# Last output tiles of part B run among the prepass's first chains, later loads of fresh stores, and the gate values in fewer transfers

## The chip, the core and the metric

The kernel runs on one core of one Trainium2 chip. The metric is device microseconds of one execution, as the median over several runs; less is better. The core has a matmul engine (TensorE, PE in the profile, with its weight loads as PEld), three engines for elementwise work (VectorE, DVE; ScalarE, ACT; GpSimd, POOL), and SyncE (SP), which here only issues DMA transfers. ACT issues some transfers too. On each engine's queue instructions start in order: one that waits holds up all behind it.

## The reference

Two attention layers over the same x (2048 positions, 640 features) are mixed by a gate, g*a + (1-g)*b.

```python
g = sigmoid((x * gate_w).sum(-1, keepdims=True))
# A: 32 heads of 192, a memory of 8 rows carried from segment to segment
for s in range(64):
    h = concat([mem, x[:, 32*s:32*s+32]])
    q, k, v = h @ Wq, h @ Wk, h @ Wv            # 640 -> 32 x 192 each
    p = softmax(where(mask, q @ k.T * 192**-0.5, -1e9))
    o = einsum('bhte,hed->btd', p @ v, Wo)
    mem, out = o[:, :8], o[:, 8:]
# B: 32 heads of 20, each position looks at 8 positions, 2 apart
q, k, v = split(x @ wqkv)
p = softmax(where(idx >= 0, q . k[pos - 2*w] * 20**-0.5, -1e9))   # w = 0..7
b = (p . v[pos - 2*w]) @ wo
return g * a + (1 - g) * b
```

Inputs and weights are bf16.

## The kernel before

The program runs in three stages. **Part B** (`part_b`, L91 to L465) computes the local attention, scales its output by 1-g and stores it in DRAM (`bsc_dram`), for part A to add. The **prepass** (`prepass`) projects the rows that part A needs of all 64 segments at once (zTi, the last 8 positions of each segment) with the weights of part A and stores them (`zpk_dram`). **Part A** then goes through the 64 segments one after the other.

*Part B* works in five blocks of 484 positions (the last has 112). A block has eight steps, each for one group g of four heads; the last block has two steps of four groups each. A step makes the scores on PE (L260) from `bqkT`, the exponentials on ACT (L267), the band mask on DVE (L276), then, one step later, the sums and values on PE (`ps_bZ`, `ps_bO`, L292), their reciprocal as two activations on ACT (L305, L306), and the product on DVE (L324), which after each four groups is stored to `bo_dram` by four transfers (L328).

Between these, jobs for the next block are taken: transposes of x (`xT_chain`, L160), the gate (`gate`, which also loads the next x tiles), projections to q and k (`proj`, L227; evacuated to `bqkD`, four buffers; stored to `bqk_dram`, L234), projections to v (`v_chain`, L210), and output chains of the block before (`out_chain`, L345). q and k come back in another layout through DRAM: `load_qk` (L243) reads `bqk_dram` into `bqkT`, half a block by four transfers. The attention output goes the same way: `load_o` (L333) reads `bo_dram` into `OT`, and an `out_chain` for one tile `ti` of 128 positions and one half `f` of the features is five matmuls of 128x320, an evacuation with the factor 1-g (`omg_sb`; ACT for f=0, L348; DVE for f=1, L350) into `bo` (two buffers), and after f=1 a store to `bsc_dram` (L352). There are 16 tiles, so 32 chains.

The gate values go through DRAM as well: `g_sb` to `g_dram` (L375), then four loads to `gA` (L385) and sixteen loads of 32x1 to `gZ` (L390), two transfers after each step from block 2 on.

In part B the order on PE, ACT, DVE and SP is the order in which the code records it (`manual_schedule`). On SP stand besides the above: early weights of part A (`wres_*`, L538), copies of some weights in DRAM (`wscr`, L524), and the first segment. PE has eight banks of PSUM; part B uses two for jobs (`b_psm`), four for scores and two for `ps_bO` and `ps_bZ`.

*Between part B and the prepass*, `load_late(0)` asks on SP for thirty weight slices (13 `wlate_k`, 16 `wlate_v`, one `wlate_oa`, 384 KB each, L538). From here a scheduler places the instructions in each engine's order.

*The prepass* calls `project_qk` four times (p = 0 to 3). Each has 24 chains of five matmuls 128x512 (L583), evacuated in turn by ACT (L77) and DVE (L79) into `ZS`, which one transfer on ACT's queue stores (L587, 3072 KB). ZS lies in the pool `zs0` for p = 0 and 2, in `zs1`, on the right side of SBUF, for p = 1 and 3. Then `project_v` (L595) with stores at L604. The prepass takes PSUM from a pool of eight banks.

PSUM and SBUF pools are freed and taken again; an instruction that writes to space of a closed pool waits for what still uses it.

Of the kernel before, what the change touches and what calls it, by code (L numbers as in the profile page):

```python
# [27 lines left out]
class _K:  # L28
# [61 lines left out]
    def part_b(self):  # L90
# [9 lines left out]
        self.xh_dram = self.dram.tile([S // 32, 128, KC * 32], BF, name="xh_dram")  # L100
        self.gA = self.const.tile([128, 4 * self.NT], F32, name="gA")
        self.gZ = self.const.tile([128, 4], F32, name="gZ")
        with ExitStack() as ctx:
            wp = ctx.enter_context(tc.tile_pool(name="b_w", bufs=1))
            io = ctx.enter_context(tc.tile_pool(name="b_io", bufs=4))
            blkp = ctx.enter_context(tc.tile_pool(name="b_blk", bufs=1))
            wk = ctx.enter_context(tc.tile_pool(name="b_wk", bufs=2))
            psm = ctx.enter_context(tc.tile_pool(name="b_psm", bufs=2, space=bass.MemoryType.PSUM))
            psS = ctx.enter_context(tc.tile_pool(name="b_psS", bufs=2, space=bass.MemoryType.PSUM))
            psO = ctx.enter_context(tc.tile_pool(name="b_psO", bufs=1, space=bass.MemoryType.PSUM))  # L110

# [11 lines left out]
                load_x(i)  # L123
            wv = wp.tile([128, KC, 640], BF, name="wv_sb")
            gw = wp.tile([128, KC, 1], BF, name="gw_sb")
            wo = wp.tile([128, KC, 640], BF, name="b_wo")
            wqk = [wp.tile([128, KC, 640], BF, name=f"b_w{n}") for n in "qk"]
            xT = wp.tile([128, KC, HALO + S], BF, name="xT")
            OT = wp.tile([128, KC, S], BF, name="OT")
            wsrc = self.wqkv.rearrange("(c p) f -> p c f", p=128)  # L130
            nc.sync.dma_start(wqk[0][:], wsrc[:, :, 0:640])
            nc.scalar.dma_start(wqk[1][:], wsrc[:, :, 640:1280])
# [14 lines left out]
            nc.vector.memset(xT[:, :, 0:HALO], 0.0)  # L147
            gz = wp.tile([128, self.NT], F32, name="gz_sb")
            g_sb = wp.tile([128, self.NT], F32, name="g_sb")
            omg_sb = wp.tile([128, self.NT], F32, name="omg_sb")  # L150
            sel_ones = wp.tile([128, 160], BF, name="sel_ones")
            zTi = self.zTi.rearrange("p c (i s) -> p c i s", i=8)
            heads = lambda t: t.rearrange("(g h d) n -> h d g n", h=4, d=20)
# [10 lines left out]
            def gate(b):  # L164
                t0 = 512 * b
                for i in range(4):
                    del xs[4 * b + i]
                    if 4 * b + 4 + i < self.NT:
                        load_x(4 * b + 4 + i)
                ps_g = bank(F32, "ps_g")  # L170
                for i in range(4):
                    c0 = HALO + t0 + 128 * i
                    for kc in range(KC):
                        nc.tensor.matmul(ps_g[:, i:i + 1], lhsT=xT[:, kc, c0:c0 + 128], rhs=gw[:, kc, :],
                                         start=(kc == 0), stop=(kc == KC - 1), skip_group_check=True)
                gs = slice(4 * b, 4 * b + 4)
                nc.scalar.activation(gz[:, gs], ps_g[:, 0:4], ACT.Exp, scale=-1.0)
                nc.vector.tensor_scalar_add(gz[:, gs], gz[:, gs], 1.0)
                nc.vector.reciprocal(g_sb[:, gs], gz[:, gs])
                nc.vector.tensor_scalar(out=omg_sb[:, gs], in0=g_sb[:, gs], scalar1=-1.0, scalar2=1.0,  # L180
                                        op0=ALU.mult, op1=ALU.add)
                xv = xT[:, :, HALO + t0:HALO + t0 + 512].rearrange("p c (s t) -> p s c t", t=32)
                xh = blkp.tile([128, 16, KC, 32], BF, name="xh_blk")
                nc.gpsimd.tensor_copy(xh[:, :, :, 8:32], xv[:, :, :, 0:24])
                nc.gpsimd.tensor_copy(xh[:, :, :, 0:8], xv[:, :, :, 24:32])
                xh_stores.append(lambda: nc.sync.dma_start(
                    self.xh_dram[16 * b:16 * b + 16].rearrange("s p f -> p s f"), xh[:].rearrange("p s c t -> p s (c t)")))
                z_copy = nc.gpsimd.tensor_copy(zTi[:, :, :, 16 * b:16 * b + 16],
                                               xv[:, :, :, 24:32].rearrange("p s c i -> p c i s"))
                if b == 3:  # L190
                    with tc.issue_after(z_copy.ins):
                        self.build_sel(self.const, sel_ones[:])
# [137 lines left out]
            def load_o(b):  # L330
                nq, nu, c0 = shape_of(b)
                nt = nq * nu
                load = nc.sync.dma_start(OT[:, :, BQ * b:BQ * b + nt], ot_dram[b][:].rearrange("(c p) n -> p c n", p=128))  # L333
                if b == 2:
                    self.mid_load = load.ins

# [1 line left out]

            def out_chain(ti, f):
                if f == 0:  # L340
                    bos[ti] = io.tile([128, 640], BF, name="bo", bufs=2)
                bo = bos[ti]
                ps = bank(F32, "ps_bo")
                for c in range(KC):
                    nc.tensor.matmul(ps[:, 0:320], lhsT=OT[:, c, 128 * ti:128 * ti + 128],  # L345
                                     rhs=wo[:, c, 320 * f:320 * f + 320], start=(c == 0), stop=(c == KC - 1))
                if f == 0:
                    nc.scalar.activation(bo[:, 0:320], ps[:, 0:320], ACT.Copy, scale=omg_sb[:, ti:ti + 1])  # L348
                else:
                    nc.vector.tensor_scalar(out=bo[:, 320:640], in0=ps[:, 0:320], scalar1=omg_sb[:, ti:ti + 1],  # L350
                                            scalar2=None, op0=ALU.mult)
                    nc.sync.dma_start(self.bsc_dram[ti * 128:(ti + 1) * 128, :], bo[:])  # L352
# [4 lines left out]
            with order:  # L357
# [12 lines left out]
                for u in range(4):  # L370
                    for f in range(2):
                        v_chain(0, u, f)
                    if u == 0:
                        load_qk(0, 1)
                misc, misc_g = [], [lambda: nc.sync.dma_start(g_dram[:].rearrange("u t n -> (u t) n"), g_sb[:])]  # L375

                def load_first():
                    self.hT0 = self.load_seg(0)
# [5 lines left out]
                for jj in range(4):  # L384
                    misc_g.append(lambda jj=jj: nc.sync.dma_start(  # L385
                        self.gA[32 * jj:32 * jj + 32, :].rearrange("t (u n) -> t u n", u=4),
                        g_dram[:].rearrange("u t n -> t u n")))
                for n in range(4):
                    for q in range(4):
                        misc_g.append(lambda n=n, q=q: nc.sync.dma_start(  # L390
                            self.gZ[32 * q:32 * q + 32, n:n + 1], g_dram[:, 24:32, 4 * n + q:4 * n + q + 1]))

                steps = [(b, (g,)) for b in range(NB - 1) for g in range(8)]
                steps += [(NB - 1, tuple(range(4 * n, 4 * n + 4))) for n in range(2)]
# [1 line left out]

                def add_outs(b):
                    load_o(b)
                    later.extend([lambda ti=ti, f=f: out_chain(ti, f) for ti in range(self.NT) for f in range(2)
                                  if BQ * b < 128 * (ti + 1) <= BQ * b + BQ])  # L400

                for i, (b, gs) in enumerate(steps):
                    g, nb, jobs = gs[0], b + 1, []
# [17 lines left out]
                    for _ in range(n_out.get(g, 0) if nb < NB else 1 + 2 * (i == len(steps) - 1)):  # L421
                        if outs:
                            jobs.append(outs.pop(0))
                    prev = steps[i - 1] if i else None
                    scores(b, gs, 0)
                    scores(b, gs, 1)
# [14 lines left out]
                    if g == 2:  # L441
                        while xh_stores:
                            xh_stores.pop(0)()
                    if nb < NB and g == (4 if full else 3):
                        load_qk(nb, 0)
                    if nb < NB and g == (7 if full else 4):
                        load_qk(nb, 1)
                    if g == 1 and b > 0:
                        add_outs(b - 1)
                    if nb == NB and g == 0:  # L450
                        add_outs(b - 1)
# [2 lines left out]
                    if b == 1 and misc:  # L454
                        misc.pop(0)()
                    if b >= 2 and g > 0:
                        for load in misc_g[:2]:
                            load()
                        del misc_g[:2]
                values(*steps[-1])  # L460
                recip(*steps[-1])
                norm(*steps[-1])
                load_o(NB - 1)
                for load in early + misc + misc_g:
                    load()  # L465
                for job in outs + later:
                    job()
            ti = self.NT - 1
            for f in range(2):
                out_chain(ti, f)  # L470

    def slice_keys(self):
        keys = []
# [89 lines left out]
    def prepass(self):  # L563
# [6 lines left out]
        def project_qk(p, pool):  # L570
# [6 lines left out]
            for r in range(2):  # L577
                for j in range(4):
                    for t in range(3):
                        ps = self.pst([128, NZ], F32, name="ps_pre")  # L580
                        c0 = 384 * j + 128 * t
                        for kc in range(KC):
                            nc.tensor.matmul(ps[:], lhsT=sls[r][kc][:, c0:c0 + 128], rhs=zTi[:, kc, :],  # L583
                                             start=(kc == 0), stop=(kc == KC - 1))
                        zc = 96 * r + 8 * (4 * t + j)
                        self.evac(ZS[:, :, zc:zc + 8], ps[:].rearrange("p (i s) -> p s i", i=8))
            nc.scalar.dma_start(self.zpk_dram[:, :, z0:z0 + 192].rearrange("s p f -> p s f"), ZS[:])  # L587

        def project_v(sls, R):
# [14 lines left out]
                    nc.scalar.dma_start(dst, ZV[64 * (k % 2):64 * (k % 2) + 64, :].rearrange("s (j f) -> s j f", j=4))  # L604

        zTi = self.zTi
        with tc.tile_pool(name="pre_zs1", bufs=1, side="right", reuse_waits="tile") as zs1:
            with tc.tile_pool(name="pre_zs0", bufs=1, reuse_waits="tile") as zs0:
                project_qk(0, zs0)
                project_qk(1, zs1)  # L610
                project_qk(2, zs0)
            project_qk(3, zs1)
# [421 lines left out]
def kernel(  # L1034
# [18 lines left out]
    k.evac_pat = "ad"  # L1053
    k.part_b()
    k.load_late(0)
    with tc.tile_pool(name="psum", bufs=8, space=bass.MemoryType.PSUM) as k.psum:
        with tc.issue_after(k.mid_load):
            k.prepass()
    k.last_loads = k.load_late(3, wait=True)
    k.part_a()  # L1060

# [30 lines left out]
```

## Time and profile before

| | |
|---|---|
| median of 3 runs | 1739.38 us (1737.59 to 1740.66) |
| profiled execution | 1740.24 us, of which the span of the instructions is 1738.4 |
| PE, ACT, DVE busy in the span | 1636.9 (94%), 861.1 (50%), 633.4 us (36%) |
| mean granted clock of PE | 0.987 |
| part B | 0 to about 204 us |
| prepass | 204 to about 364 us |
| part A | about 364 us to the end |

PE's busy time in windows of 50 us is 39.50, 43.51, 41.80 and 32.73 in part B, and 48 and more in the prepass. The granted clock is the share of full speed that the throttle gave PE. In timelines a line has the start in us, the length, the engine (with q behind it for issues of transfers), the line of the kernel, the operation, the tile written and the tiles read, their sizes and the number of instructions; in brackets stand the idle time before it and what ended that.

### The profile page before, as it was taken

To read this page: it belongs to the slowest core of one execution; us is meant where nothing else is said; L and a number is where in the kernel's file an instruction comes from. 1 tells how busy PE (TensorE), PEld (TensorE's weight loads), DVE (VectorE), ACT (ScalarE), POOL (GpSimd) and SP (SyncE) were. 2 spreads that over 40 slices of the span, in tenths; PEclk is the share of its full clock that TensorE was granted. 3 is DMA by queue.
4 is the path that set the end of the run, shared out by engine and by line. 5 is a ranking of instruction groups with operands and counts; after the bars stand their busy time and mean duration, and the time that the engine had idled before them with its cause. 6 is when DMAs were issued, how large, how long until landed. Compare 5 with 4: busy or idle time off the path is not lost.

```text
span 1738.4 us, 82021 instructions
## 1 busy us (share of the span) xinstructions
PE 1636.9 (94%) x36266; PEld 974.0 (56%) x36281; DVE 633.4 (36%) x2027; ACT 861.1 (50%) x2338; POOL 59.5 (3%) x124
## 2 busy tenths in 40 slices
PE   7887799999999999999999999999999999999989
PEld 4544344445555555556556555555555555555557
DVE  3665233233333333333333333333333333333330
ACT  3887322235555555555555555555555455555550
POOL 2030000000000000000000000000000000000000
PEclk9998899999999999999999999999999999999999
DMA  7887697889999999999899999999999989999991
GB/s 199 224 200 193 209 289 186 252 265 298 299 307 299 295 295 305 302 299 309 296 295 304 300 299 291 298 301 297 294 294 299 301 285 298 302 291 299 295 294 31
DMA packets 299313, 477.46 MB, mean 275 GB/s; under 512 B 99789, under 2 KB 176077, under 8 KB 298957
## 3 DMA queue, kind: packets, MB, share of 16 engines
q1 hardware_dynamic: 200544, 416.58, 74.2%
q10 hardware_dynamic: 98412, 55.64, 11.4%
q8 instruction: 283, 4.64, 1.1%
q14 instruction: 74, 0.60, 0.1%
HBM read 430.40 MB, written 44.48 MB: 273 GB/s over the span
## 4 chain that ended last, share of the span: by engine, by line
PE 86%; DMA 5%; ACT 4%; issue 3%; DVE 1%; ACTq 1%; SPq 1%; DVEq 0%
PE ps_qk L710 25%; PE ps_v L803 13%; PE ps_wo L867 12%; PE ps_pre L583 6%; PE ps_qkT L727 6%; PE ps_S L757 5%; PE ps_oT L826 3%; PE ps_z L1024 3%; PE ps_pre L595 2%; PE ps_bqk L227 2%; ACT ZB L951 2%; PE ps_mem L877 1%; PE ps_S L766 1%; DMA wst<-in_A_Wv_dram 1%; PE ps_S L786 1%
## 5 line engine op out<-in xcount | busy, mean ns | idle before, releaser
L719 ACT CAST TZ<-ps_qk 128x384 bf16<-128x384 f32 x448 | 208.2, 479 | 334.7 <-PE ps_qk L710 187.0
L710 PEld LDWEIGHTS <-hT 128*32 128x32 bf16 x10240 | 245.9, 96 | 157.6 <-issue 15.1
L710 PE MATMUL ps_qk<-wres_q,hT 128*32 128x384 bf16 x4096 | 225.5, 327 | 5.6 <-issue 4.1
L734 DVE COPY ZB<-ps_qkT 128x384 bf16<-128x384 bf16 x256 | 91.6, 358 | 379.3 <-PE ps_qkT L727 215.3
L803 PE MATMUL ps_v<-wlate_v,hT 128*32 128x384 bf16 x4096 | 225.0, 329 | 0.0
L710 PE MATMUL ps_qk<-wlate_k,hT 128*32 128x384 bf16 x3328 | 202.2, 328 | 0.0
L867 PEld LDWEIGHTS <-TZ 128*32 128x32 bf16 x6144 | 155.0, 96 | 69.5 <-issue 21.4
L710 PE MATMUL ps_qk<-wst,hT 128*32 128x384 bf16 x1792 | 153.3, 328 | 1.1 <-issue 0.5
L803 PEld LDWEIGHTS <-hT 128*32 128x32 bf16 x5120 | 113.9, 96 | 69.4 <-issue 6.6
L867 PE MATMUL ps_wo<-wlate_oa,TZ 128*32 128x384 bf16 x2560 | 141.0, 327 | 5.2 <-issue 5.2
L757 PE MATMUL ps_S<-ZB,TZ 128*128 128x160 bf16 (+1 forms) x1024 | 136.8, 238 | 0.0
L867 PE MATMUL ps_wo<-wlate_ob,TZ 128*32 128x256 bf16 x2688 | 124.4, 275 | 7.9 <-issue 7.8
L727 PE MATMUL ps_qkT<-ident,TZ 128*128 128x128 bf16 x1536 | 129.9, 221 | 0.9 <-ACT TZ L719 0.9
L727 PEld LDWEIGHTS <-TZ 128*128 128x128 bf16 x1536 | 88.9, 98 | 61.7 <-issue 40.2
L775 ACT ACTIVATE ZB<-ps_S 32x224 bf16<-32x224 f32 x256 | 89.0, 348 | 42.8 <-PE ps_S L766 40.5
L837 DVE CAST TZ<-ps_oT 128x192 bf16<-128x192 f32 x256 | 79.6, 352 | 63.7 <-PE ps_oT L831 63.4
L837 ACT CAST TZ<-ps_oT 128x192 bf16<-128x192 f32 x256 | 69.7, 327 | 58.1 <-PE ps_oT L831 58.1
L757 PEld LDWEIGHTS <-TZ 128*128 128x128 bf16 (+1 forms) x1024 | 58.8, 95 | 68.1 <-issue 40.0
L880 DVE CAST hT<-ps_mem 128x24 bf16<-128x24 f32 x126 | 22.6, 179 | 203.9 <-PE ps_mem L877 203.9
L810 ACT CAST TZ<-ps_v 128x384 bf16<-128x384 f32 x192 | 92.3, 481 | 3.1
L803 PE MATMUL ps_v<-wst,hT 128*32 128x384 bf16 x1024 | 87.0, 330 | 5.2 <-DMA wst<-in_A_Wv_dram 5.2
L775 ACT ACTIVATE TZ<-ps_S 32x224 bf16<-32x224 f32 x256 | 88.7, 347 | 2.3
(134 smaller groups left out, 2231.8 us busy)
## 6 DMA issues: line engine op xcount, KB each, us to landing
wst<-in_A_Wq_dram SPq DMA_DIRECT2D x260, 384.0 KB
wst<-in_A_Wv_dram SPq DMA_DIRECT2D x260, 384.0 KB
wst<-in_A_Wk_dram SPq DMA_DIRECT2D x195, 384.0 KB
wst<-wscr SPq DMA_DIRECT2D x192, 384.0 KB
zpk_dram<-ZS ACTq DMA_DIRECT2D x4, 3072.0 KB
ZB<-zpk_dram ACTq DMA_DIRECT2D x64, 192.0 KB
wres_q<-in_A_Wq_dram SPq DMA_DIRECT2D x16, 384.0 KB
wlate_v<-in_A_Wv_dram SPq DMA_DIRECT2D x16, 384.0 KB
```

The lines of the kernel that those rows point to most:

```text
L583: nc.tensor.matmul(ps[:], lhsT=sls[r][kc][:, c0:c0 + 128], rhs=zTi[:, kc, :], start=(kc == 0), stop=(kc == KC - 1))
L710: nc.tensor.matmul(pq[32 * j:32 * j + 32, 0:384], lhsT=hT[:, kc, :], rhs=sl[:, 384 * j:384 * j + 384], start=(kc == 0), stop=(kc == KC - 1 ...
L719: cp(sts[i], pqs[i][:, 0:384])
L727: nc.tensor.transpose(pT[:, t, :, :, :].rearrange("p j b i -> p (j b i)"), st[:, 128 * t:128 * t + 128], self.ident[:])
L734: nc.vector.tensor_copy(q_blocks(R)[:, 1:5, :, :].rearrange("p b c i -> p c b i"), pT.rearrange("p t j b i -> p (t j) b i"))
L757: nc.tensor.matmul(grid(h, par)[:, :, 0:80].rearrange("p j (b r i) -> p j b r i", r=2, i=8)[:, :, :, r, :], lhsT=KT[k0:k1, 12 * r + c:12 * ...
L775: nc.scalar.activation(E[ps], pSs[h][ps, :, 112 * j:112 * j + 112], ACT.Exp, scale=scale_a)
L803: nc.tensor.matmul(pvs[R][32 * j:32 * j + 32, 0:384], lhsT=hT[:, kc, :], rhs=sl[:, 384 * j:384 * j + 384], start=(kc == 0), stop=(kc == KC ...
L810: cp(V[R], pvs[R][:, 0:384])
L826: nc.tensor.matmul(out[:, r, t, :], lhsT=V[2 * h + r][ks, f0:f1], rhs=E[ks, par, 0:80].rearrange("p (b r i) -> p b r i", r=2, i=8)[:, :, r ...
L837: cps[j % 2](oTxs[2 * h + j // 2][:, 6 * (j % 2):6 * (j % 2) + 6, :], pos[j][:, 0:240].rearrange("p (c q) -> p c q", q=40)[:, :, 8:40])
L867: nc.tensor.matmul(pso[part][32 * jj:32 * jj + 32, 0:n], lhsT=oTxs[2 * (R // 2) + j // 2][:, 6 * (j % 2) + 3 * (R % 2) + t, :], rhs=o_weig ...
```

## The change

The last five output tiles (11 to 15, ten chains) aren't run in part B: they are kept as `tail_outs`, and one is taken after each of the chains 7 to 16 of the first `project_qk`. What they need (`wo`, `omg_sb`, `bo`, now with three buffers, and `OT_last`, the part of OT from position 1408 on) moves to a pool of its own, `b_out`, on the right side of SBUF, which is closed after the first `project_qk`; `zs1` is opened after that. Their PSUM, `b_psm`, is kept until the end of the prepass, whose own pool has six banks instead of eight.

In part B, `load_qk` for a block's first half is asked for one step later, for the second half at the first step of the block itself instead of the last step of the block before; `load_o` one step later; the six jobs of block 3's first step (two projections of q and k each, two output chains) get another order. For the last block the loads move to steps 4 and 5.

The gate values are copied to `gq_sb` by DVE, once per block, stored to `gz_dram` by four small transfers, and loaded to `gZ` by one; the transfers for gA and gZ are issued one per step instead of two.

```diff
         self.gZ = self.const.tile([128, 4], F32, name="gZ")
+        self.out_ctx, self.out_ps = ExitStack(), ExitStack()
+        outp = self.out_ctx.enter_context(tc.tile_pool(name="b_out", bufs=1, side="right"))
+        psm = self.out_ps.enter_context(tc.tile_pool(name="b_psm", bufs=2, space=bass.MemoryType.PSUM))
         with ExitStack() as ctx:
...
             wk = ctx.enter_context(tc.tile_pool(name="b_wk", bufs=2))
-            psm = ctx.enter_context(tc.tile_pool(name="b_psm", bufs=2, space=bass.MemoryType.PSUM))
             psS = ctx.enter_context(tc.tile_pool(name="b_psS", bufs=2, space=bass.MemoryType.PSUM))
...
             gw = wp.tile([128, KC, 1], BF, name="gw_sb")
-            wo = wp.tile([128, KC, 640], BF, name="b_wo")
+            wo = outp.tile([128, KC, 640], BF, name="b_wo")
             wqk = [wp.tile([128, KC, 640], BF, name=f"b_w{n}") for n in "qk"]
             xT = wp.tile([128, KC, HALO + S], BF, name="xT")
-            OT = wp.tile([128, KC, S], BF, name="OT")
+            T_LAST = 11
+            SPLIT = 128 * T_LAST
+            OTs = [wp.tile([128, KC, SPLIT], BF, name="OT"), outp.tile([128, KC, S - SPLIT], BF, name="OT_last")]
             wsrc = self.wqkv.rearrange("(c p) f -> p c f", p=128)
...
             g_sb = wp.tile([128, self.NT], F32, name="g_sb")
-            omg_sb = wp.tile([128, self.NT], F32, name="omg_sb")
+            omg_sb = outp.tile([128, self.NT], F32, name="omg_sb")
+            gq_sb = wp.tile([128, self.NT], F32, name="gq_sb")
             sel_ones = wp.tile([128, 160], BF, name="sel_ones")
...
                                         op0=ALU.mult, op1=ALU.add)
+                nc.vector.tensor_copy(gq_sb[:].rearrange("p (q n) -> p q n", q=4)[:, :, b:b + 1],
+                                      g_sb[:, gs].rearrange("p (n q) -> p q n", q=4))
                 xv = xT[:, :, HALO + t0:HALO + t0 + 512].rearrange("p c (s t) -> p s c t", t=32)
...
                 nt = nq * nu
-                load = nc.sync.dma_start(OT[:, :, BQ * b:BQ * b + nt], ot_dram[b][:].rearrange("(c p) n -> p c n", p=128))
+                for n, OT in enumerate(OTs):
+                    lo, hi = max(BQ * b, SPLIT * n), min(BQ * b + nt, S if n else SPLIT)
+                    if lo < hi:
+                        load = nc.sync.dma_start(OT[:, :, lo - SPLIT * n:hi - SPLIT * n],
+                                                 ot_dram[b][:, lo - BQ * b:hi - BQ * b].rearrange("(c p) n -> p c n", p=128))
                 if b == 2:
...
                 if f == 0:
-                    bos[ti] = io.tile([128, 640], BF, name="bo", bufs=2)
+                    bos[ti] = outp.tile([128, 640], BF, name="bo", bufs=3)
                 bo = bos[ti]
...
                 for c in range(KC):
-                    nc.tensor.matmul(ps[:, 0:320], lhsT=OT[:, c, 128 * ti:128 * ti + 128],
+                    n = ti >= T_LAST
+                    t0 = 128 * ti - SPLIT * n
+                    nc.tensor.matmul(ps[:, 0:320], lhsT=OTs[n][:, c, t0:t0 + 128],
                                      rhs=wo[:, c, 320 * f:320 * f + 320], start=(c == 0), stop=(c == KC - 1))
...
                         load_qk(0, 1)
-                misc, misc_g = [], [lambda: nc.sync.dma_start(g_dram[:].rearrange("u t n -> (u t) n"), g_sb[:])]
+                misc, misc_g = [], []
+                gz_dram = self.dram.tile([4, 4, 8, 4], F32, name="gz_dram")
+                misc_g.append(lambda: nc.sync.dma_start(g_dram[:].rearrange("u t n -> (u t) n"), g_sb[:]))
+                for u in range(4):
+                    misc_g.append(lambda u=u: nc.sync.dma_start(
+                        gz_dram[:, u].rearrange("q i n -> i q n"),
+                        gq_sb[32 * u + 24:32 * u + 32].rearrange("p (q n) -> p q n", q=4)))
 
...
                         g_dram[:].rearrange("u t n -> t u n")))
-                for n in range(4):
-                    for q in range(4):
-                        misc_g.append(lambda n=n, q=q: nc.sync.dma_start(
-                            self.gZ[32 * q:32 * q + 32, n:n + 1], g_dram[:, 24:32, 4 * n + q:4 * n + q + 1]))
+                misc_g.append(lambda: nc.sync.dma_start(self.gZ[:], gz_dram[:].rearrange("q u i n -> (q u i) n")))
 
...
                     load_o(b)
-                    later.extend([lambda ti=ti, f=f: out_chain(ti, f) for ti in range(self.NT) for f in range(2)
-                                  if BQ * b < 128 * (ti + 1) <= BQ * b + BQ])
+                    if b < 3:
+                        later.extend([lambda ti=ti, f=f: out_chain(ti, f) for ti in range(T_LAST) for f in range(2)
+                                      if BQ * b < 128 * (ti + 1) <= BQ * b + BQ])
 
...
                             jobs.append(outs.pop(0))
+                    if nb == NB - 1 and g == 0 and len(jobs) == 6:
+                        jobs = [jobs[k] for k in (0, 1, 4, 2, 3, 5)]
                     prev = steps[i - 1] if i else None
...
                             xh_stores.pop(0)()
-                    if nb < NB and g == (4 if full else 3):
+                    if nb < NB and g == (5 if full else 4):
                         load_qk(nb, 0)
-                    if nb < NB and g == (7 if full else 4):
+                    if g == 0 and 0 < b < NB - 1:
+                        load_qk(b, 1)
+                    if nb == NB - 1 and g == 5:
                         load_qk(nb, 1)
-                    if g == 1 and b > 0:
+                    if g == 2 and b > 0:
                         add_outs(b - 1)
...
                     if b >= 2 and g > 0:
-                        for load in misc_g[:2]:
+                        for load in misc_g[:1]:
                             load()
-                        del misc_g[:2]
+                        del misc_g[:1]
                 values(*steps[-1])
...
                     load()
-                for job in outs + later:
+                for job in outs:
                     job()
-            ti = self.NT - 1
-            for f in range(2):
-                out_chain(ti, f)
+            self.tail_outs = [lambda ti=ti, f=f: out_chain(ti, f) for ti in range(T_LAST, self.NT) for f in range(2)]
 
...
                         self.evac(ZS[:, :, zc:zc + 8], ps[:].rearrange("p (i s) -> p s i", i=8))
+                        if p == 0 and 12 * r + 3 * j + t >= 6 and self.tail_outs:
+                            self.tail_outs.pop(0)()
             nc.scalar.dma_start(self.zpk_dram[:, :, z0:z0 + 192].rearrange("s p f -> p s f"), ZS[:])
...
         zTi = self.zTi
-        with tc.tile_pool(name="pre_zs1", bufs=1, side="right", reuse_waits="tile") as zs1:
+        with ExitStack() as zc1:
             with tc.tile_pool(name="pre_zs0", bufs=1, reuse_waits="tile") as zs0:
                 project_qk(0, zs0)
+                self.out_ctx.close()
+                zs1 = zc1.enter_context(tc.tile_pool(name="pre_zs1", bufs=1, side="right", reuse_waits="tile"))
                 project_qk(1, zs1)
...
     k.load_late(0)
-    with tc.tile_pool(name="psum", bufs=8, space=bass.MemoryType.PSUM) as k.psum:
+    with tc.tile_pool(name="psum", bufs=6, space=bass.MemoryType.PSUM) as k.psum:
         with tc.issue_after(k.mid_load):
             k.prepass()
+    k.out_ps.close()
     k.last_loads = k.load_late(3, wait=True)
```

## The prediction

> **What bounds the kernel now.** I read the table of engines first: TensorE (PE) is busy 94% of the 1738.4 us span, so a change of this size can pay only where PE idles. A table of windows finds the place: below, length, then busy us (and instructions) of PE, weight loads, DVE, ACT, POOL, the granted clock, the DMA share and GB/s.
>
> ```profile
> 150.00:200.00 50.00, 32.73 (x631) 20.65 (x631) 22.99 (x42) 30.50 (x50) 0.00 (x0) 0.80 0.64 167
> 200.00:250.00 50.00, 48.16 (x226) 22.31 (x230) 15.48 (x23) 13.43 (x24) 0.00 (x0) 1.00 0.92 306
> ```
>
> PE idles 17 us of the 50 in which part B ends, at a clock of 0.80; the prepass from 204 us on is solid. What ends the waits inside part B is in the list of waits from 40 to 186 us (engine, tile and line, what it waited for: us in all, times, longest):
>
> ```profile
> PE ps_bS L260 <- DMA bqkT<-bqk_dram: 4.4, 5, 1.9
> ACT bo L348 <- DMA bsc_dram<-bo: 2.5, 2, 1.6
> DVE bqkD L79 <- DMA gZ<-g_dram: 2.1, 1, 2.1
> DVE bqkD L79 <- DMA bqk_dram<-bqkD: 1.1, 1, 1.1
> ACT bqkD L77 <- DMA gZ<-g_dram: 0.8, 1, 0.8
> ```
>
> All of these are transfers that SP issues: 10.9 us together. They cluster at the first step of block 3, where the exponentials on ACT slip:
>
> ```profile
> 141.06 0.98 ACT L267 ACTIVATE bP<-ps_bS 128x968 bf16<-128x968 f32 x1 [3.59 <-PE ps_bS L260]
> ...
> 148.78 1.84 ACT L267 ACTIVATE bP<-ps_bS 128x968 bf16<-128x968 f32 x2 [0.49 <-PE ps_bS L260]
> ```
>
> The step from 141.06 to 148.78 takes 7.7 us, its later neighbours 4.0 and 4.5. Then the tail, on PE's timeline (start, us, line, tiles, instructions, idle before and what ended it):
>
> ```profile
> 185.66 0.85 PE L345 MATMUL ps_bo<-b_wo,OT 128*128 128x320 bf16 x5
> 192.11 4.33 PE L345 MATMUL ps_bo<-b_wo,OT 128*128 128x320 bf16 x20 [5.59 <-DMA OT<-bo_dram]
> 198.84 4.60 PE L345 MATMUL ps_bo<-b_wo,OT 128*128 128x320 bf16 x30 [2.40 <-ACT bo L348]
> 204.23 0.38 PE L583 MATMUL ps_pre<-TZ,wres_q 128*128 128x512 bf16 x1 [0.80 <-DVE bo L350]
> ```
>
> From 186.5 (185.66 + 0.85) to 204.23 are 17.7 us in which PE does ten output chains (50 matmuls): it waits for OT, then for the two bo buffers, whose stores must land. Last, SP's queue around the prepass, and the store of the first ZS on ACT's queue:
>
> ```profile
> 186.30 0.38 SPq L333 DMA_DIRECT2D OT<-bo_dram  x1
> ...
> 214.35 16.02 SPq L538 DMA_DIRECT2D wlate_v<-in_A_Wv_dram  x16
> 247.68 0.38 SPq L538 DMA_DIRECT2D wlate_oa<-in_A_Wo_dram  x1
> ```
> ```profile
> 231.10 0.39 ACTq L587 DMA_DIRECT2D zpk_dram<-ZS  x1
> ```
>
> SP issues nothing from 230.4 to 247.68. SP's and ACT's transfers take turns on eight completion semaphores, and in the built order the wlate_oa load shares one with the ZS store, so it waited until that had landed: 16.6 us from issue. It cost nothing, because nothing urgent stood behind it.
>
> **The change, part by part.**
>
> *The tail moves into the prepass.* It removes the 17.7 us. The ten chains return between chains of the first projection at the hot price: 30 matmuls in 4.60 us with a short wait, 0.137 each once hot, 0.69 per chain, 6.9 in all; I add 0.5 for the alternation of chains. Net -10.3 (between -11 and -8: at the cold price of the 192.11 row, 0.217 a matmul, the first four chains cost 1.6 more). The chain of tile 11 needs block 3's OT, issued as part B ends and, by the before row, landing 5.8 us later (186.30 to 192.11); six prepass chains of 1.08 us (5 matmuls; 49 take 10.74 in the chain of waits) stand ahead, 6.5 us. I take +0.5 for it, bounds 0 and 1.5.
>
> *Loads that read fresh stores, asked for later; six jobs reordered; a third bo buffer; gZ by one load after four small stores instead of sixteen loads, one per step.* On SP this takes eleven issues off the queue and puts the blocking ones (load_qk, load_o, gA) where what they read has landed, so that bqk and bsc stores behind them go out in time. At most the 10.9 us of named waits and what they entail vanish (the split exponentials of block 3, and the slow clock behind each idle: up to 16 in all); at least the step of block 3 recovers: 7.7 us against 5.3 by its neighbours and its six jobs, and 7.3 against 4.2 for the step before, 5.5 together. ACT sets the floor of a step (1.84 for two exponentials, about 1.1 for L305 and L306, then evacuations), so no more can come. I take -11. The four gq copies lie on DVE beside other work, which is idle for a third of each window or more; uncovered they would cost some 0.2 each, by the 179 ns of the smallest DVE cast on the page.
>
> *zs1 now lies where wo, OT_last, omg and bo lay.* This is where the stall goes. zs1 was free from the start; now ACT and DVE may write the first ZS of project_qk(1) only when tile 15's bsc store has landed. That store is the last in a queue. In the built order of the changed kernel SP has, after part B: the late loads, the 28th of which waits for the first ZS store (the same shared semaphore as before, now two places earlier), two more loads, the stores of tiles 12, 13 and 14, three wst loads, and the store of tile 15. The evacuation of tile 15 itself waits for the store of tile 12, whose buffer it takes, on ACT behind the ZS store's issue. So two bsc stores in series stand behind the whole ZS store. Counted from PE's end of the first projection, P: ZS store issued at +1.0; landed 15 later (16.6 in the row above; 12.8 if no load is in flight, since 3,146 KB at the 287 GB/s of the row below, where the loads have drained, are 11 us, plus about 2 to start; 15 since fewer loads are left now); then three issues of 0.4, and tile 12's store landing behind three loads:
>
> ```profile
> 225.00:230.00 5.00, 4.95 (x24) 2.28 (x24) 1.38 (x2) 1.69 (x3) 0.00 (x0) 1.00 1.03 400
> ...
> 240.00:245.00 5.00, 5.00 (x25) 2.25 (x23) 1.38 (x2) 1.76 (x3) 0.00 (x0) 1.00 1.26 287
> ```
> ```profile
> 171.55 2.87 DMA bsc_dram<-bo
> ...
> 186.78 5.71 DMA bsc_dram<-bo
> ```
>
> The second fence, from the chain of waits, prices a bsc store at 2.9 to 5.7; I take 4.3 each, 8.6 for two, with the 0.6 evacuation between them and 0.6 for the first evacuation after. That is 1.0 + 15 + 1.2 + 8.6 + 0.6 + 0.6 = P + 27.0. PE meanwhile fills the six banks it now has, 6 x 1.08 = 6.5. Stall: 20.5 us (lowest 12.8 and 2.9 twice: 15.5; highest 16.6 and 5.7 twice: 25). After it PE starts cold: the 192.11 row took 4.33 for 20 matmuls after a 5.6 us idle, 1.6 over the hot price, so +1.5. Behind the stalled stores stand the wst loads for the later projections, but these are asked for one projection ahead.
>
> Beside this a sentence of the Trainium skill, "DMA: Bandwidth & Descriptors", section "Anatomy of one DMA — SWDGE (gpsimd) path": a transfer takes about 2.0 us plus its bytes at 436 GB/s. For the ZS store an estimate from that page is 9.2 us, which would make the stall 5.8 shorter and the whole change come out near 1733, toward rival A. The page speaks of GpSimd's queue, and this case's rows (16.6 us, and 287 GB/s with the loads gone) differ; I go by the rows.
>
> *Small ones.* Six banks instead of eight in the later prepass: +0.5 (bounds 0 and 2; ACT and DVE wait for PE there, not PE for them). Twelve ps_qk matmuls of part A run inside the stall: -0.7 (from -1 to 0). Part A's first wst of Wv is waited for 3.16 us at 377.94 and is now issued before the wlate_ob loads: -1.5 (-3 to 0).
>
> *Sum:* -10.3 + 0.5 - 11 + 20.5 + 1.5 + 0.5 - 0.7 - 1.5 = **-0.5 us**. Against the profiled execution (span 1738.4, 1740.24 in all) that is 1739.7; the median of the runs is 0.86 lower, so **1738.9**.
>
> **The rivals.**
>
> A: *the stall is short and part B gains its upper bound.* For it: SP drains earlier relative to the ZS store than before, since the first projection is 7 us longer. Against: two serial stores stay. Stall 16 and gain 15 give -0.5 - 4.5 - 4 = -9: **1730**.
>
> B, slower: *ACT and the slow clock pace part B, not SP.* Over 150:200 PE's clock is 0.80 and ACT is busy 30.5 of 50; steps in which no DMA is named still take 3.7 to 4.5 us. Then only block 3's 5.5 come back while the stall stays: -0.5 + 5.5 = +5, to +9 with the stall at 24; **1745**. It decides if the named waits are worth less than 7 us. For it: most idle of ACT in part B is put down to PE, not to a transfer. Against: the chain of waits runs through SP from 130 to 146 us.
>
> C: *SP stays late.* The bqkT loads now stand behind more stores of the same step and may be as late as before at block 3; gain in part B 6 at most, spent again on the OT wait: **1744**.
>
> **Chances.** Forecast 0.46, within 1734 to 1744; A 0.22; B 0.22; C 0.10. A measurement of this kernel can tell about 0.2% (3.5 us) from no change. The forecast splits 0.10 faster, 0.25 same, 0.11 slower; A is faster; B 0.20 slower, 0.02 same; C 0.07 and 0.03. So faster 0.32, same 0.30, slower 0.38. The range runs from A (1730, 2 lower for its bounds) to B with a long stall (1748.5).
>
> **What would show it.** Right: the first prepass chain some 27 to 30 us earlier than 204.23; no bqkT wait above 1 us on L260; in the first projection ps_bo chains at 0.69; then one idle of PE of 15 to 25 us before the seventh chain of the second projection, ended by ACT or DVE, whose own waits name bsc_dram; the span's later course only shifted. Wrong: no such idle (then the time is near 1717), or a first prepass chain later than 181.

## The result and the profile after

The changed kernel is slower: a median of 1758.87 us (1755.42 to 1760.19, four runs) against 1740.01 (1737.59 to 1740.66, four runs), a ratio of 1.0108 with a 95% interval of 1.0089 to 1.0127. The profiled execution took 1755.42 us, its span is 1753.6, so 15.2 more than the span before. Line numbers after the change are higher by 7 in part B's steps (scores L267), by 13 in `out_chain` (L358; stores L365) and by 19 to 23 later on (prepass L602, part A L733).

The table of windows of the changed kernel (columns as before):

```profile
150.00:200.00 50.00, 42.09 (x730) 25.23 (x724) 26.14 (x47) 33.25 (x54) 0.00 (x0) 0.86 0.62 153
200.00:250.00 50.00, 27.14 (x140) 13.01 (x139) 7.18 (x11) 6.17 (x11) 0.00 (x0) 0.81 0.98 333
```

The hole at the end of part B is filled (PE busy 42.1 of 50 where it was 32.7), and a larger one has opened in the prepass (27.1 where it was 48.2). On PE's timeline of the changed kernel:

```profile
184.95 0.41 PE L299 MATMUL ps_bO<-bP,bV 63*32 63x56 bf16 x32 [0.22 <-DVE boT L331]
...
186.77 0.82 PE L602 MATMUL ps_pre<-TZ,wres_q 128*128 128x512 bf16 x3 [0.63 <-DVE boT L331]
...
245.34 0.83 PE L733 MATMUL ps_qk<-wres_q,hT 128*32 128x384 bf16 x8 [19.04 <-DVE bo L363]
250.94 1.86 PE L602 MATMUL ps_pre<-TZ,wres_q 128*128 128x512 bf16 x4 [4.77 <-ACT ZS L77]
```

Three things are to be read here. The prepass begins 17.5 us earlier (186.77 against 204.23), and that is the tail. Part B itself ends where it did: its last values start at 184.95, before at 185.33. And in the second projection PE idles 19.04 + 4.77 = 23.8 us. The name behind the first part, a `bo` evacuation, is that of tile 15. SP's and ACT's queues of the changed kernel tell why it came so late:

```profile
207.47 32.01 SPq L557 DMA_DIRECT2D wlate_v<-in_A_Wv_dram  x16
239.52 0.43 SPq L557 DMA_DIRECT2D wlate_oa<-in_A_Wo_dram  x1
240.06 1.39 SPq L365 DMA_DIRECT2D bsc_dram<-bo  x3
241.50 2.32 SPq L557 DMA_DIRECT2D wst<-in_A_Wk_dram  x3
245.35 0.33 SPq L365 DMA_DIRECT2D bsc_dram<-bo  x1
```
```profile
220.63 0.39 ACTq L608 DMA_DIRECT2D zpk_dram<-ZS  x1
244.64 0.53 ACT L361 ACTIVATE bo<-ps_bo,omg_sb 128x320 bf16<-128x320 f32 x1 [25.27 <-DMA bsc_dram<-bo]
250.31 1.56 ACT L77 CAST ZS<-ps_pre 128x512 bf16<-128x512 f32 x3 [5.14 <-DMA bsc_dram<-bo]
```

The sixteen `wlate_v` issues, 16.02 us before, now span 32.01: the last two come only when the ZS store, issued at 220.63, has landed. Right behind them, at 240.06, the three bsc stores of tiles 12 to 14 go out; ACT gets its buffer for tile 15 at 244.64; tile 15's store goes out at 245.35; at 250.31 the first ZS of the second projection may be written. And in part B (list of waits from 40 to 186 us, as shown of before):

```profile
PE ps_bS L267 <- DMA bqkT<-bqk_dram: 7.5, 9, 1.3
...
```

The waits for gZ and for bsc stores are gone, but the wait for bqkT, 4.4 us before, is 7.5.

### The profile page after: what moved, and what is told of

It is laid out like the page before. It is cut to its first block, busy times and chain, and to the rows that moved or that the text cites. A ratio compares the mean times of both kernels' runs of the same rounds, so it can differ in the third digit from the quotient of the medians.

```text
span 1753.6 us, 82021 instructions
## 1 busy us (share of the span) xinstructions
PE 1641.4 (94%) x36281; PEld 983.4 (56%) x36281; DVE 630.7 (36%) x2031; ACT 860.8 (49%) x2338; POOL 60.1 (3%) x124
## 4 chain that ended last, share of the span: by engine, by line
PE 85%; DMA 6%; ACT 3%; issue 3%; DVE 1%; ACTq 1%; SPq 0%; DVEq 0%
PE ps_qk L733 25%; PE ps_v L826 13%; PE ps_wo L890 12%; PE ps_qkT L750 6%; PE ps_pre L602 6%; PE ps_S L780 5%; PE ps_oT L849 3%; PE ps_z L1047 3%; PE ps_pre L616 3%; PE ps_bqk L234 2%; DMA bqkT<-bqk_dram 2%; ACT ZB L974 2%; PE ps_mem L900 1%; PE ps_S L789 1%; PE ps_bo L358 1%
## 5 line engine op out<-in xcount | busy, mean ns | idle before, releaser
L733 PEld LDWEIGHTS <-hT 128*32 128x32 bf16 x10240 | 245.8, 96 | 178.4 <-issue 35.4
L733 PE MATMUL ps_qk<-wres_q,hT 128*32 128x384 bf16 x4096 | 226.3, 328 | 22.9 <-DVE bo L363 19.0
L733 PE MATMUL ps_qk<-wlate_k,hT 128*32 128x384 bf16 x3328 | 202.4, 328 | 0.0
L733 PE MATMUL ps_qk<-wst,hT 128*32 128x384 bf16 x1792 | 153.2, 328 | 2.2 <-issue 1.4
```

The costliest lines, as they stand in the source:

```text
L733: nc.tensor.matmul(pq[32 * j:32 * j + 32, 0:384], lhsT=hT[:, kc, :], rhs=sl[:, 384 * j:384 * j + 384], start=(kc == 0), stop=(kc == KC - 1 ...
```

## The experiments

Each kernel ran beside the kernel before on the same chip. The ratios are to that, with 95% intervals. The kernel before spread from 1724 to 1749 us in these sessions, so small effects are read from ratios, and of profiles only waits and orders. Programs that are alike up to the end of part B end it up to 6.7 us apart in their profiled executions (its last values start at 183.71 in e2 and at 190.38 in e9), so where part B ends in a single profile shows little.

**Taking the two suspects of the changed kernel apart.** e1 puts load_qk back:

```diff
-                    if nb < NB and g == (5 if full else 4):
+                    if nb < NB and g == (4 if full else 3):
                         load_qk(nb, 0)
-                    if g == 0 and 0 < b < NB - 1:
-                        load_qk(b, 1)
-                    if nb == NB - 1 and g == 5:
+                    if nb < NB and g == (7 if full else 4):
                         load_qk(nb, 1)
```

> The changed kernel with load_qk asked for where the kernel before asked for it, everything else as changed. Theory T (the loads of bqkT, asked for one step later, land after the block needs them, which spends what the other changes of SP's queue win in part B): the waits of L267 for bqkT fall from 8.0 us to 4 or less, part B ends 4 to 8 us earlier than in the changed kernel (PE's last matmul of part B at 178 to 182 instead of 186.1), the time 1751 to 1755. Rival P (ACT and PE's clock pace part B, no order of SP's queue matters): part B ends within 1 us of 186.1, time 1758 to 1760.

Measured 1.0086 (1.0058 to 1.0114); the waits of L267 for bqkT (from 30 to 187 us) fell from 8.0 to 1.3 us, part B's last values began at 179.09, 5.9 earlier, and the idle in the second projection stayed (19.87 + 4.41). The late loads cost something, and the rival "ACT paces part B" is not what this trace shows; but the ratios of this run and of the changed kernel overlap, so this run alone does not size it, and 5.9 us are within what programs with the same part B differ by.

e2 moves the last five tiles' stores to another queue:

```diff
-                    nc.sync.dma_start(self.bsc_dram[ti * 128:(ti + 1) * 128, :], bo[:])
+                    eng = nc.scalar if ti >= T_LAST else nc.sync
+                    eng.dma_start(self.bsc_dram[ti * 128:(ti + 1) * 128, :], bo[:])
```

> The changed kernel with the bsc stores of the tiles 11 to 15 issued on ACT's queue instead of SP's. Theory S (the 23.8 us idle of PE in the second projection is the two bsc stores standing on SP behind late loads that wait for the ZS store): the idle goes altogether or shrinks to under 3 us; ACT may lose 1 to 4 us to waits for shared semaphores; time 1734 to 1741. Rival B (six banks and the space that zs1 takes over are the cause, whichever queue stores): an idle of 10 us or more stays in the second projection, time 1745 or more.

Measured 0.9975 (0.9955 to 0.9995): a little faster than the kernel before. The window of e2 in which the changed kernel had its hole:

```profile
200.00:250.00 50.00, 49.66 (x247) 23.29 (x245) 16.15 (x24) 13.77 (x24) 0.00 (x0) 1.00 0.98 322
```

PE is busy 49.7 of 50 at full clock, with the same six banks and zs1 on the same space. From 1.0108 to 0.9975 are 1.3%, some 23 us: the whole stall.

**The changes of part B without the tail.** e3 is the kernel before with gZ's new transfers, load_o later and the new order of jobs; e4 the kernel before with only load_qk later (e1's diff the other way round).

> The kernel before, with the changes of SP's queue in part B but for load_qk: load_o one step later, the six jobs of block 3's first step in the new order, gZ by one load after four stores, one transfer for the gate values per step. No output tile is moved. Theory T: part B ends 3 to 8 us earlier than before (186.5), time 1732 to 1737. Rival P: part B ends within 1 us of 186.5, time 1739 to 1741.

> The kernel before with load_qk asked for as in the changed kernel, nothing else. Theory T: the waits for bqkT grow from 5.0 us to 8 or more, part B ends 3 to 8 us later, time 1743 to 1748. Rival P: the waits move to other engines and the time stays within 2 us of the 1740.

e3 came out at 0.9985 (0.9967 to 1.0003), less than Theory T wanted, with 1 inside the interval; e4 at 1.0041 (1.0022 to 1.0060), some 7 us slower. How the two act is seen in the first steps of the blocks. SP's issue of block 3's first bqkT and PE's wait for it: first the kernel e3, then the changed kernel (its first two lines are waits in blocks 1 and 2), then e4.

```profile
128.09 1.89 SPq L246 DMA_DIRECT2D bqkT<-bqk_dram  x4
```
```profile
66.31 0.22 PE L267 MATMUL ps_bS<-bqkT 20*128 20x121 bf16 x1 [1.27 <-DMA bqkT<-bqk_dram]
...
107.43 0.39 PE L267 MATMUL ps_bS<-bqkT 20*128 20x121 bf16 x7 [1.07 <-DMA bqkT<-bqk_dram]
...
136.19 1.70 SPq L250 DMA_DIRECT2D bqkT<-bqk_dram  x4
...
141.89 0.23 PE L267 MATMUL ps_bS<-bqkT 20*128 20x121 bf16 x1 [0.60 <-DMA bqkT<-bqk_dram]
```
```profile
145.81 0.28 PE L260 MATMUL ps_bS<-bqkT 20*128 20x121 bf16 x1 [4.10 <-DMA bqkT<-bqk_dram]
```

Part B does not reach block 3 at the same time in these runs, so the issues are counted from the start of the last exponentials of block 2 on ACT (133.77 before, 131.78 in e3, 137.45 in the changed kernel, 137.87 in e4). Before, the four loads went out at 135.06, 1.3 us after that, and PE waited 4.0 us for them in all. In e3, with SP relieved, they go out 3.7 us ahead of it and no wait is left in block 3. In the changed kernel SP is relieved as well, but the loads are recorded one step later and go out 1.3 ahead: half of what the relief had won is spent, and 2.5 us of waits are left. The growth from 4.4 to 7.5 us is not at block 3 but at blocks 1 and 2, where the waits are 5.1 us against 0.4 before. In e4, without the relief, the loads go out 3.4 us after the exponentials; PE waits 4.10 us for the first of them, 5.9 in block 3 and 5.5 in blocks 1 and 2, 11.4 in all from 40 to 186 us.

e7 is gZ's change alone (gq_sb, gz_dram, one transfer per step):

> The kernel before with the gate values copied to gq_sb, stored to gz_dram by four transfers and loaded to gZ by one, one transfer for the gate values per step; nothing else. If the sixteen loads of gZ are what makes SP late at block 3, part B ends 3 us or more earlier than 186.5 and the ratio is 0.996 to 0.999; if load_o and the order of jobs are, part B ends within 1 us of 186.5 and the ratio is 0.999 to 1.001.

Measured 0.9972 (0.9947 to 0.9996), with PE's waits for bqkT from 30 to 187 us down to 3.7 us (5.0 before) and its last values of part B 1.6 earlier (183.69). The ratio is in the band of the first alternative and the end of part B is between the two; e3 and e7 cannot be told apart. So the new handling of the gate values is the part of the gain that is shown, and no ratio shows one from load_o or the order of jobs. Which part of that handling it was stays open, because the edit also halves the pace of these transfers. SP's queue of the kernel before shows what stood ahead of block 3's loads:

```profile
119.74 0.43 SPq L375 DMA_DIRECT2D g_dram<-g_sb  x1
125.05 0.32 SPq L385 DMA_DIRECT2D gA<-g_dram  x1
...
132.38 0.73 SPq L390 DMA_DIRECT2D gZ<-g_dram  x1
...
135.06 1.69 SPq L243 DMA_DIRECT2D bqkT<-bqk_dram  x4
```

Only one of the sixteen gZ loads was out by then. The first load of gA had held SP for 4.9 us, until the store to g_dram that it reads had landed. In e7 the first gA load goes out at 139.92, behind block 3's first loads (131.12), and that wait is gone.

**The tail alone.** e6 is the kernel before with only the ten chains moved:

> The kernel before with the ten output chains moved (tail_outs, pools, six banks, third bo buffer), and nothing of SP's queue in part B changed. Theory T: the effects add up, so that what part B gained and lost in the changed kernel is absent here: part B ends at 184 to 187, the idle in the second projection is 20 to 25 us, ratio 1.008 to 1.013. Rival: without the other changes SP is late, the late loads come later against the ZS store, and the idle differs by over 4 us from 23.8.

Measured 1.0091 (1.0059 to 1.0122), idle 19.92 + 3.56 = 23.5 us, the first ZS of the second projection written 29.4 us after the first ZS store's issue, in the changed kernel 29.7. The stall belongs to the move of the tail and does not depend on part B's queue. The effects add up: 1.0091 x 0.9985 x 1.0041 = 1.0117, measured together 1.0108.

**What sets the stall.** e5 asks for four of the thirty late loads only behind the first projection:

```diff
-    k.load_late(0)
+    k.late_rest = k.load_late(0, wait=True)
+    for load in k.late_rest[:26]:
+        load()
+    del k.late_rest[:26]
...
                 project_qk(0, zs0)
+                for load in self.late_rest:
+                    load()
                 self.out_ctx.close()
```

> The changed kernel with only 26 of the thirty late loads asked for before the prepass, the other four behind the first project_qk. In the built order the store of tile 12 then stands ahead of the transfer that waits for the first ZS store (now the store of tile 13), so that the evacuation of tile 15 waits for nothing on SP and one bsc store instead of two stands behind the ZS store. Theory S (two stores in series behind the ZS store): the idle of PE in the second projection, 23.8 us, shrinks by one store, to 17 to 20 us; time 4 to 7 us under the changed kernel, ratio to the kernel before 1.006 to 1.009. Rival B (banks and space alone): the idle stays within 1 us of 23.8, ratio 1.010 to 1.012. Rival Q (only the order of late loads against the stores counts, not the ZS store): nothing is late any more, idle under 5 us, ratio under 1.000.

Measured 1.0090 (1.0058 to 1.0122). The idle is 3.48 + 20.83 = 24.3 us, as the rival had it and not as mine. PE's and SP's timelines of e5:

```profile
230.94 0.51 PE L735 MATMUL ps_qk<-wres_q,hT 128*32 128x384 bf16 x8 [3.48 <-DVE bo L363]
252.28 1.86 PE L602 MATMUL ps_pre<-TZ,wres_q 128*128 128x512 bf16 x4 [20.83 <-ACT ZS L77]
```
```profile
223.41 17.68 SPq L365 DMA_DIRECT2D bsc_dram<-bo  x3
241.13 1.41 SPq L557 DMA_DIRECT2D wlate_v<-in_A_Wv_dram  x3
242.59 0.43 SPq L557 DMA_DIRECT2D wlate_oa<-in_A_Wo_dram  x1
243.07 1.57 SPq L557 DMA_DIRECT2D wst<-in_A_Wk_dram  x3
244.74 0.47 SPq L365 DMA_DIRECT2D bsc_dram<-bo  x1
```

The edit did what it was to do: tile 12's store is out at 223.41, tile 15 is evacuated at 230.24, and now it is the store of tile 13 that waits for the ZS store (issued at 221.80). But tile 15's store still stands behind it, with seven loads in between, and goes out at 244.74, 22.9 us after the ZS store's issue; in the changed kernel it was 24.7 (220.63 to 245.35). It then takes 6.9 us until ZS may be written (251.64), behind seven loads; before 5.0, behind three. One store in series less was paid back by four loads more ahead of the other.

e9 uses the same edit with 13 instead of 26, which in the built order puts all four stores ahead of the load that waits for the ZS store:

> The changed kernel with 13 of the thirty late loads asked for before the prepass and the other 17 behind the first project_qk. The stores of the tiles 12 to 15 stay on SP, zs1 stays where it is, six banks stay; but in the built order all four stores now stand ahead of the transfer that waits for the first ZS store. Theory S2 (the stall is the place of the stores on SP, behind a load that waits for the ZS store; not the number of stores in series, not banks or space): idle of PE in the second projection under 3 us, ratio to the kernel before 0.996 to 1.000 as with the stores on ACT's queue (0.9975). Rival B (banks and space): idle 15 us or more, ratio over 1.006.

Measured 0.9968 (0.9944 to 0.9991). SP's and PE's timelines of e9:

```profile
214.32 2.30 SPq L365 DMA_DIRECT2D bsc_dram<-bo  x3
217.22 1.32 SPq L557 DMA_DIRECT2D wlate_v<-in_A_Wv_dram  x2
222.28 0.33 SPq L365 DMA_DIRECT2D bsc_dram<-bo  x1
222.65 26.90 SPq L557 DMA_DIRECT2D wlate_v<-in_A_Wv_dram  x14
```
```profile
236.84 1.02 PE L602 MATMUL ps_pre<-TZ,wres_q 128*128 128x512 bf16 x4 [0.34 <-DVE ZS L79]
```

The stores are on the same queue, zs1 on the same space, the banks are six: the idle is 0.34 us. Together with e2, which leaves SP's loads as they are, that leaves the place of the stores on SP, behind what waits for the ZS store, as the cause.

**Versions that beat both kernels.** e8 has both repairs (e1 and e2), e10 the repairs of e1 and e9, e11 that of e9 and the first half's load_qk alone.

> The changed kernel with both repairs: the bsc stores of tiles 11 to 15 on ACT's queue, and load_qk asked for where the kernel before asked for it. If the two effects are independent, the ratio to the kernel before is that of the first repair alone (0.9975) less what the second gave in the changed kernel (1.0108 to 1.0086, 0.2 to 0.4%): 0.992 to 0.996. If the gain of part B is given back in the prepass, the ratio stays at 0.997 to 0.999.

> As e9, and load_qk asked for where the kernel before asked for it. If the effects are independent, the ratio is 0.991 to 0.996, as with the stores on ACT's queue (0.9914); waits for bqkT in part B 4 us or less.

> As e9, and only the first half's load_qk of each block asked for where the kernel before asked for it; the second half's stays later. In the traces so far all waits for bqkT stand at the first step of a block. If only the first half is needed early, ratio within 0.002 of e10; if the second half matters too, new waits for bqkT appear at the fifth step of a block and the ratio lies nearer to e9.

e8: 0.9914 (0.9882 to 0.9946), e10: 0.9921 (0.9889 to 0.9954), e11: 0.9929 (0.9901 to 0.9957). The repairs add up, by either way of getting the stores out; e8 came out just under its band. Asking for load_qk one step later thus costs 0.22% (changed kernel against e1), 0.41% (e4), 0.47% (e9 against e10) and 0.61% (e2 against e8). The profiles fit: with load_qk late (changed kernel, e2, e5, e9) the last values of part B start at 186.3 on average and PE's waits for bqkT are 6.8 to 10.1 us from 30 to 187 us; with it early (e1, e8, e10, e12) at 181.7, with waits of 1.3 to 2.6. In e11 block 3 has no wait at its first step, but 0.40 + 0.85 + 0.94 us at its fifth, for the second half's bqkT, asked for at 150.30: the second half's load is late there too, though the ratio does not show it.

Last, a residue: with six banks PE idles 3.25 us in `project_v` in the changed kernel and 3.30 in e2, where before it was 0.93. e12 is e10 with eight banks from there on:

```diff
             project_qk(3, zs1)
+        self.ps_ctx.close()
+        self.out_ps.close()
+        self.psum = self.ps_ctx.enter_context(tc.tile_pool(name="psum8", bufs=8, space=bass.MemoryType.PSUM))
```

> As e10 (stores ahead on SP, load_qk early), and after the fourth projection the six banks and part B's two are closed and a pool of eight opened for project_v and what follows. In all kernels with six banks so far PE idles 3.3 us in project_v where the kernel before idles 0.93. If six banks are the cause, that idle falls to 1.5 us or less and the ratio to 0.989 to 0.993 (e10: 0.9921); if it comes from the delayed weight loads or ACT, it stays above 3 us and the ratio stays. Against it: closing the pools may cost a wait of its own, up to 2 us, at the start of project_v.

That idle on PE's timeline in e2:

```profile
316.21 4.91 PE L617 MATMUL ps_pre<-wlate_v,TZ 128*128 128x512 bf16 x11 [3.30 <-ACT ZV L77]
```

In e12 PE does not idle there at all: the banks were the cause. A new idle of 0.79 us stands at the start of `project_v` (297.69), until the last ZS is evacuated; which fits the cost of closing the pools that was expected at up to 2 us. The ratio, 0.9915 (0.9886 to 0.9945), is that of e10 within the intervals; in the same execution the wait for part A's first wst of Wv rose to 3.47 us (1.59 in e10), so a part may have been given back there. That was not followed further.

## Why the prediction was wrong

1. *The tail, -10.3.* Right in size: of the 17.7 us between part B's last matmul and the prepass 17.1 went (186.14 to 186.77 is left), and the chains came back at about the hot price: 24 of their 50 matmuls, on PE at 193.26, took 3.61 us, 0.15 each where I had 0.137. That makes some 9.6 net.
2. *"Loads that read fresh stores, asked for later ...": -11.* **This is the step that failed.** The two halves of it have opposite signs: without load_qk the changes of SP's queue give 0.9985, load_qk later costs 1.0041, together 1.0026, or +4.5 us on 1740 (by their intervals about 0 to 9). In the profiled executions part B's last values start only 0.4 us earlier than before. The prediction's own signs of being wrong there are met: the first prepass chain is later than 181 (186.77), and a wait for bqkT is above 1 us (1.3). I took the list of waits for a list of what SP's blocking issues cost, and added up its lines as if every cause would go. But a wait for bqkT has two prices: how late SP gets to the load, and how long the load itself takes until PE can use it. Asked for at 135.06 and used from 139.47 on, the row before showed some 4.4 us for the second, which no relief of SP removes and which a later request makes visible, at blocks 1 and 2 above all, where SP had not been late. Nor did the relief alone give what the list promised: e3 took the waits for bqkT from 4.4 to 0.9 us and those for gZ away, for 0.15%, some 2.6 us. What made SP late at block 3 was the handling of the gate values (e7); one piece of it, gA's 4.9 us, was a load that waited for its fresh store, as the prediction had it. Rival C had this mechanism, priced as a gain of part B that is lost, not as a loss; rival B (ACT and clock as the pace) is not borne out: e3's and e1's waits for bqkT, 0.9 and 1.3 us, leave a part B that ends 4.6 and 5.9 us earlier than in its counterpart, though programs with the same part B differ by as much in single executions.
3. *The stall, +20.5.* Mechanism right, size within its bounds (15.5 to 25): 23.8. The ZS store's landing released SP near 239, 18 us after its issue, where I had 15, and the row that I had set aside as too high, 16.6, was nearer. I had reckoned with fewer loads in flight beside it; in the trace the loads moved more than the store until 5.9 us after its issue, against 3.9 before. "Two bsc stores in series" was a poor way to size the rest: e5 shows that removing one changes nothing when more loads stand ahead of the other. By the estimate of 9.2 us from the Trainium skill, "DMA: Bandwidth & Descriptors", section "Anatomy of one DMA — SWDGE (gpsimd) path", whose fit is for GpSimd's queue, the ZS store would have landed sooner; the trace disagrees, by a factor of about two, for this store on ACT's queue with loads beside it.
4. *Six banks, +0.5 (0 to 2).* Too small, and above its bound: the idle grew by 2.3 us (3.25 against 0.93), and e12 shows that it is the banks.
5. *OT wait, cold clock, moved ps_qk, wst:* the tile 11 chains had no wait for OT_last; after the stall the first four matmuls took 1.86 us where four take 1.03; the wst wait fell by 1.1 us (3.16 to 2.06).

With +4.5 for -11, 23.8 for 20.5 and 2.3 for 0.5, the recorded sum of 1738.9 becomes 1759.5; measured was 1758.9. That it closes so well is in part luck, since part B's 4.5 is known only to some 4 us either way. The range failed because the two rivals that had part B wrong ended at "no gain", and none at a loss, though the later load was in the change itself.

## What to carry to other kernels

A load moved later must be priced twice: what it frees on its queue, and how long before its first use it now starts. Where buffers pass to another owner, find the last transfer that still reads them, follow it through its whole queue, and look for anything ahead of it there that waits for something slow, as here a load for the ZS store. The fix may be an order (13 loads instead of 30 ahead of four stores, 23 us) and cost nothing. A list of waits names causes; it isn't a sum of gains.

## What the hardware showed that was not expected

The ZS store of 3072 KB moved little while late loads were in flight, and the profile's view of the DMA queues, taken in short stretches, shows how. Before the change the store was issued at 231.10, and up to 234.5 its queue moved no packet while SP's moved 501 (1.37 MB). In the changed kernel, issued at 220.63, it moved none up to 224; from 224 to 226 it moved 252 packets and the loads 254, but that was 0.10 MB against 0.69. In e9 it is the same from 231 to 235: 491 packets and 499, 0.19 MB and 1.37. So the two queues got about as many packets each, and the store, with packets of 384 bytes beside the loads' 2.7 KB, a seventh of the bytes. Once the loads were done it ran alone at 287 to 290 GB/s, and landed 16.6 us (before) and 18 us (changed kernel) after its issue.
